# Turning q, k and x of eight head pairs by SyncE's transposing transfers instead of TensorE, with clamping sums, shared MLP sums and a new order of work

## The chip, the cores and the metric

The kernel runs on one core of one Trainium2 chip. A core has TensorE (matrix products, written to PSUM, eight banks of 2 KB per partition), VectorE, ScalarE, GpSimd and SyncE, each with an instruction queue of its own that it works off in order. In the profile they are PE, DVE, ACT, POOL and SP; PEld is TensorE's weight load. GpSimd and SyncE also issue the transfers (DMAs), which sixteen DMA engines carry out. The metric is the device time of one execution in microseconds (us).

## The reference

Windowed attention with eight global keys, followed by a token mixer of low rank and an MLP, for 4 batches, 8 heads, 768 tokens and 64 values per head:

```
scores = q @ k.T / sqrt(D) - slope[h] * dist      # keep: key < 8, or 0 <= query - key < 96
a = exp(scores - max); a = a / sum(a);  x = a @ v  # [4, 768, 512], heads side by side
u = x + (x.T @ U @ V).T                            # U is 768 x 32, V is 32 x 768
out = u + relu(u @ w_ch1) @ w_ch2                  # 512 -> 2048 -> 512
```

## The kernel before, in words

**Pairs.** The 32 heads are taken as 16 pairs p, four for each batch b (p = 4b + hp). A pair fills 128 partitions: two heads of 64 values.

**Attention of a pair** (function attention, line 578). GpSimd loads q, k and v as 16-bit numbers with tokens on the partitions (lq, lk, lv; three buffers for q and for k, four for v). TQ and TK turn q and k to values on the partitions: six 128x128 transposes each on TensorE (flip, line 611; for pairs 0 to 3 another form in line 592), into a PSUM bank. EQ and EK copy the banks to qT and kT (three buffers each), on ScalarE or VectorE as the tables "EQ" and "EK" say by a letter for each pair (A ScalarE, D VectorE, S SyncE, Q a transfer of GpSimd). KO makes kO, the keys shifted for the window, VC and VG do the same for v (SyncE for pairs 7 to 11 and 13 to 15, with one and two transfers). S forms the scores in up to three parts, EX takes exp, MK multiplies the mask, PV multiplies with v, RC and NM divide by the sum and write x as 32-bit numbers to x_sb.

**Mixer of a pair.** XC casts x to 16 bits (x16). UP (mixed, line 835) has six blocks of 128 tokens: for each, one product with the identity, which lays x transposed into two PSUM banks (line 840), and one with U of 32 columns (line 845). XE copies the 32 columns, XU turns them (line 948), TE copies them to tmp, HM (line 966) multiplies with V and adds onto the transposed x in the two banks, so that they hold u transposed. E0 copies them to uT, on the engine of table "E"; for the last pair of a batch E1 (ScalarE) and E0 (VectorE) take half each.

**MLP of a batch** (function mlp, line 995). The first product, 512 to 2048, has sixteen blocks jt of 128. Plain blocks (M1 with RL, RM) are four products of 384 or 768 columns and a relu on ScalarE. Blocks z of CFG["Z"] (4 to 7 in batches 1 and 2, 2 to 7 in batch 3) are done with block z + 8 by seven products in place of eight (ZP1 to ZP7, line 1115): ZT forms sums of uT, ZS sums of w1 (lines 1093 to 1096, four operations of 256 elements for each z, kept for z = 4 to 7, made anew in batch 3 for 2 and 3), ZU, ZW, ZX copy partial results to zu on ScalarE, ZA, ZB and ZD add a bank and such a copy on VectorE (tt, line 1133), ZR is a relu from PSUM, and ZQ and ZV are relus in place behind ZA, ZD and ZB (flat_relu, lines 1172 and 1174). The second product, 2048 to 512, is done by seven products in place of eight too: PA and PB form sums of its input (sA, two VectorE operations each, lines 1199 to 1205), RS starts three token blocks, P1 to P7 multiply (line 1246, eight products of 256 columns for each), DA, DB, DC, DD, DF and DG add banks onto x_sb (lines 1258, 1298), O stores the result (SyncE).

**What sets the order.** ORDER (line 21) names every step once, by hand. A planner (line 106) walks through it with a cost for each step, gives out buffers and PSUM banks, and sorts the steps by the start that it works out; on each engine they run in the order of the list. Semaphores between the engines follow from the data.

The lines that turn and mix x, and those that let it go on:

```
nc.tensor.matmul(ps[:, gx.slot + c // 3, ...], xx[:, c], ident16, ...)          # L840
nc.tensor.matmul(ps[:, gx.slot, 384:384 + R], xx[:, c], u16[:, c, 0], ...)      # L845
ut_done[p] = (add(e, ..., ev, [HM] + w, rel=[gx], name=f"E0{p}"),)              # copy to uT
```

## Time and profile before

| | |
|---|---|
| device time, median of 3 runs (lowest to highest) | 224.5 us (224.15 to 225.14) |
| profiled execution: span from first to last instruction | 223.0 us; the page records no other time of it |
| TensorE busy, instructions | 216.4 us, 2424 |
| VectorE busy | 181.6 us, 403 |
| ScalarE busy | 147.0 us, 260 |
| GpSimd busy | 73.7 us, 97 |
| granted TensorE clock | full throughout |
| GpSimd's transfers | 13.74 MB in 72880 packets |
| SyncE's transfers | 9.19 MB in 14496 packets |

Busy times of TensorE are of pipelined products, whose lengths overlap: six transposes of 0.22 us take 0.34 us together. In the chain of work and the timeline a merged piece therefore gives the time that its products hold TensorE, and the starts of single products give their pace. The attention of batch 0 runs from 0 to about 36 us, its MLP, mixed with the attention of batch 1, to about 80 us; the later first and second MLP products lie at 80 to 107 and 107 to 131 us (batch 1), 131 to 157 and 157 to 180 us (batch 2), 180 to 201 and 201 to 220 us (batch 3), with the attention of the next batch between.

### The profile page before, as it was taken

Reading aid. Unit: us, or ns where it says so; the run is one execution under the profiler, and the core shown is the slowest. Engines: PE = TensorE matmul, PEld = TensorE weight load, DVE = VectorE, ACT = ScalarE, POOL = GpSimd, SP = SyncE. Lnnn points to the kernel's source line nnn. Section 1 sums busy time; section 2 is a strip of 40 time slices with the busy share of each in tenths; the row PEclk is TensorE's granted clock in tenths of the full one; section 3 lists DMA queues with packets and bytes.
Section 4 is the critical chain, followed back from the end, with each engine's and each line's share of the span. In section 5 each row is a group of like instructions: output and inputs, shape, how many; then the busy total and the mean of one; then the engine's idle time right before and its main releaser. Section 6 shows DMA issues by size and latency. Waiting matters only on the chain.

```text
span 223.0 us, 5965 instructions
## 1 busy us (share of the span) xinstructions
PE 216.4 (97%) x2424; PEld 158.5 (71%) x2424; DVE 181.6 (81%) x403; ACT 147.0 (66%) x260; POOL 73.7 (33%) x97
## 2 busy tenths in 40 slices
PE   8799899999999999999999999999999999999994
PEld 3466656675879976666888876666788875658883
DVE  5688966999987987888978688597978796889872
ACT  7888798768858669788757557787742458782000
POOL 8989959714894940010851000011000000000000
PEclk9999999999999999999999999999999999999999
DMA  6999999999999997662997021409100006000025
GB/s 173 178 170 149 159 161 185 184 206 166 158 157 92 140 191 141 224 46 37 68 116 98 18 79 65 132 4 71 33 0 3 0 3 259 25 1 3 0 97 190
DMA packets 87404, 23.31 MB, mean 104 GB/s; under 512 B 73840, under 2 KB 84784, under 8 KB 87376
## 3 DMA queue, kind: packets, MB, share of 16 engines
q0 software_dynamic: 72880, 13.74, 75.6%
q1 hardware_dynamic: 14496, 9.19, 14.2%
q8 instruction: 19, 0.31, 0.6%
q14 instruction: 9, 0.07, 0.1%
HBM read 27.56 MB, written 6.29 MB: 152 GB/s over the span
## 4 chain that ended last, share of the span: by engine, by line
PE 84%; DMA 7%; POOL 5%; issue 2%; DVE 1%; ACT 0%; DVEq 0%; POOLq 0%
PE ps L1246 34%; PE ps L1115 14%; PE ps L1020 11%; PE ps L1044 7%; PE ps L734 4%; DMA vt<-in_v_dram 4%; PE ps L611 3%; DMA stgq<-in_q_dram 3%; PE ps L840 2%; PE ps L867 2%; PE ps L866 2%; POOL stgq L457 1%; POOL w L507 1%; PE ps L1238 1%; PE ps L966 1%
## 5 line engine op out<-in xcount | busy, mean ns | idle before, releaser
L799 ACT ACTIVATE ep<-ps 128x1024 f16<-128x1024 f32 (+1 forms) x48 | 44.0, 952 | 16.3 <-PE ps L734 15.1
L1246 PEld LDWEIGHTS <-htr 128*128 128x128 f16 x392 | 36.2, 98 | 6.1 <-issue 1.9
L1020 PE MATMUL ps<-uT,w 128*128 128x384 f16 x176 | 33.3, 326 | 0.0
L1258 DVE TENSOR_TENSOR x_sb<-x_sb,ps 128x256 f32<-128x256 f32 (+1 forms) x60 | 26.8, 463 | 7.6 <-PE ps L1246 7.2
L1246 PEld LDWEIGHTS <-sA 128*128 128x128 f16 x288 | 27.4, 98 | 4.2 <-issue 0.7
L461 POOL DMA_DIRECT2D vt<-in_v_dram x16 | 16.7, 1047 | 32.9 <-PE ps L867 29.7
L1026 ACT ACTIVATE htr<-ps 128x384 f16<-128x384 f32 x44 | 20.7, 493 | 5.6 <-PE ps L1020 5.3
L1246 PE MATMUL ps<-w,sA 128*128 128x256 f16 x192 | 24.2, 273 | 0.0
L1246 PE MATMUL ps<-tB,htr 128*128 128x256 f16 (+1 forms) x200 | 24.2, 268 | 0.0
L1020 PEld LDWEIGHTS <-w 128*128 128x128 f16 x176 | 16.5, 98 | 10.6
L1246 PE MATMUL ps<-w,htr 128*128 128x256 f16 x192 | 23.5, 273 | 0.0
L457 POOL DMA_DIRECT2D stgq<-in_q_dram x24 | 19.9, 852 | 5.4 <-PE ps L611 3.3
L1044 PE MATMUL ps<-uT,w 128*128 128x384 f16 x112 | 21.3, 326 | 0.0
L457 POOL DMA_DIRECT2D stgk<-in_k_dram x24 | 20.0, 852 | 2.6 <-DMA w<-in_moe_w_ch_dram 1.0
L1133 DVE TENSOR_TENSOR htr<-ps,zu 128x384 f16<-128x384 f32 x30 | 16.4, 553 | 4.7 <-PE ps L1115 3.0
L362 ACT ACTIVATE zu<-ps 128x384 f32<-128x384 f32 x30 | 14.7, 493 | 5.7 <-PE ps L1115 5.3
L812 DVE TENSOR_TENSOR ep<-ep,mask 128x1024 f16<-128x1024 f16 x24 | 16.2, 684 | 1.4 <-ACT ep L799 0.9
L905 DVE TENSOR_TENSOR x_sb<-ps,rcp 128x768 f32<-128x768 f32 x16 | 15.3, 956 | 0.9 <-DMA vo<-vt 0.4
L1044 PEld LDWEIGHTS <-w 128*128 128x128 f16 x112 | 10.7, 98 | 6.6
L1115 PEld LDWEIGHTS <-w 128*128 128x128 f16 x108 | 10.2, 98 | 6.1
L734 PE MATMUL ps<-qT,kT 64*128 64x128 f16 x192 | 14.0, 217 | 0.4 <-DVE kT L364 0.4
L1115 PE MATMUL ps<-uT,w 128*128 128x384 f16 x56 | 13.4, 326 | 0.0
(124 smaller groups left out, 450.0 us busy)
## 6 DMA issues: line engine op xcount, KB each, us to landing
out_dram<-x_sb SPq DMA_DIRECT2D x20, 256.0 KB, 2.2
vt<-in_v_dram POOLq DMA_DIRECT2D x16, 192.0 KB, 5.9
stgk<-in_k_dram POOLq DMA_DIRECT2D x24, 96.0 KB, 6.6
stgq<-in_q_dram POOLq DMA_DIRECT2D x24, 96.0 KB, 5.6
w<-in_moe_w_ch_dram POOLq DMA_DIRECT2D x8, 256.0 KB, 7.1
w<-in_moe_w_ch_dram POOLq DMA_DIRECT2D x4, 512.0 KB, 11.7
vo<-vt SPq DMA_DIRECT2D x8, 123.8 KB, 2.5
out_dram<-x_sb SPq DMA_DIRECT2D x7, 128.0 KB, 2.2
```

Of the source, the lines that this page charges most:

```text
L457: nc.gpsimd.dma_start(o[:, i], src[b, h0 + i].rearrange("(n p) d -> p n d", p=P))
L461: nc.gpsimd.dma_start(vt[gv.slot][:, :, :, 0:D], v[b, h0:h0 + 2].rearrange("h (n p) d -> p h n d", p=P),)
L734: nc.tensor.matmul(t[:, hi, j * P:(j + 1) * P], lhs, qt[r, i * P:(i + 1) * P], start=not biased, stop=True, skip_group_check=biased,)
L799: nc.scalar.activation(ep[gep.slot][:, :, lo:512], ps[:, gsc.slot:gsc.slot + 2, lo:512], AF.Exp, scale=qk_scale)
L812: nc.vector.tensor_tensor(ev, ev, mv, ALU.mult)
L1020: nc.tensor.matmul(ps[:, g.slot, 0:HS], w1[:, dc, jt * P:(jt + 1) * P], ub[:, dc, i * HS:(i + 1) * HS], start=(dc == 0), stop=(dc == NDC - 1),
L1026: nc.scalar.activation(htr[:, jt, i * HS:(i + 1) * HS], ps[:, g.slot, 0:HS], AF.Relu)
L1044: nc.tensor.matmul(ps[:, g.slot + half, 0:HS], w1[:, dc, jt * P:(jt + 1) * P], ub[:, dc, half * HS:(half + 1) * HS], start=(dc == flat[0]) ...
L1115: nc.tensor.matmul(bank(g), a()[:, i], bq[:, i], start=first and i == 0, stop=last and i == 1, skip_group_check=True,)
L1133: return lambda: nc.vector.tensor_tensor(o, x(), y(), ALU.add)
L1246: nc.tensor.matmul(o if part is None else o[:, part], a[:, j, c0 + cols.start:c0 + cols.stop], bq[:, j] if part is None else bq[:, j, part ...
L1258: nc.vector.tensor_tensor(o, o, x, ALU.add)
```

## The change

- **q and k of pairs 8 to 15** (CFG["QD"]): TQ and TK fall away; EQ and EK become one transposing transfer each, issued by SyncE from the loaded tile straight to qT or kT.
- **x of pairs 8 to 15** (CFG["XD"]): UP keeps its six products with U and loses the six with the identity. A transposing transfer XT, issued by SyncE behind XC, writes x transposed to uT. HM starts its banks afresh, and E0 (with E1 for pairs 11 and 15) adds the bank onto uT in place, always on VectorE, behind HM and XT.
- **Clamping sums**: ZA, ZB and ZD become one VectorE operation that adds and clamps from below at 0; ZQ and ZV fall away.
- **MLP sums**: ZS is made once for two blocks z (four operations of 512 elements, three steps ZS1 to ZS3), and kept; the third lies where ib and early were, so it waits for the last bias step SB.
- **PA and PB** become Sa, Sb, Sc and Sd, one operation each, and each product waits only for the one that it reads.
- **A new ORDER** and other letters in the tables of engines. Options that were switched off are taken out.

```diff
--- before.py
+++ after.py
-from concourse.masks import make_identity
+from concourse.dve_ops import TENSOR_ADD_SAT
...
 ORDER
...
+HM4 RS0.2 P20.2 E04 lv7 lk12 lq7 lq8 lv6 Sb0.3 EK7 Sd0.3 KO7 Sb0.0 lk8 lq9 lk9 VG5 Sb0.1 Sd0.0 Sd0.1 P50.0 S6.1 P20.0
+P50.2 EX6.1 PV5 EX6.2 TQ7 P30.0 P30.2 EQ7 MK6.0 VC6 RC5 NM5 lv10 S7.1 MK6.1 MK6.2 Sc0.1 DF0.2 DF0.0 P10.0 P10.2 EK8
+mask6 VG7 VC7 VG6 EQ8 XC5 EX7.2 PV6 EX7.1 RS0.1 EQ9 S7.0 DA0.0 DC0.2 TWb0 EK9 P10.1 RC6 DA0.1 DA0.2 P20.1 P50.1 P60.0
+KO8 EX7.0 MK7.1 NM6 S8.1 P30.1 P60.2 EX8.2 EX8.1 XC6 MK7.2 MK7.0 DB0.0 Sc0.3 DC0.0 DB0.2 DF0.1 UP5 PV7 RC7 XE5 NM7
+P70.2 XU5 P60.1 S8.0 TE5 HM5 DD0.2 MK8.2 E05 lq11 lv8 lk10 DB0.1 P70.0 lq10 P40.2 lk11 lq12 EX8.0 lv9 DD0.0 DC0.1 ZS2
+XC7 UP7 XE7 UP6 XE6 P70.1 XU7 DD0.1 DG0.2 XU6 TE7 P40.0 TE6 KO9 HM7 HM6 DG0.0 E17 E06 P40.1 E07 S9.1 DG0.1 EX9.1 S9.0
...
+lk13 PV10 Sb1.0 Sb1.3 DA1.1 MK11.1 DA1.0 RC10 Sd1.3 Sd1.1 NM10 Sc1.1 P61.1 P51.0 Sc1.2 VC14 P61.0 DB1.0 Sc1.0 Sd1.0
+XC10 P51.1 S12.1 VG11 VC11 P21.1 EQ14 EK14 EK13 KO14 EX12.2 XC9 P31.0 P31.1 XT8 Sc1.3 DB1.1 EX12.1 MK11.2 PV11 UP9
+P71.1 KO13 XT9 DF1.1 XE9 XU9 TE9 P71.0 lv15 RC11 VC12 NM11 DF1.0 S12.0 EX12.0 HM9 RS1.2 DD1.0 P11.2 XC11 UP8 DC1.1
+DD1.1 XE8 P41.1 E09 VG14 XT10 XT11 lv13 lk15 EK15 UP10 XU8 DA1.2 MK12.2 MK12.0 P21.2 TE8 HM8 P41.0 DG1.1 XE10 XU10 E08
+TE10 DC1.0 P61.2 UP11 HM10 P31.2 DB1.2 XE11 XU11 P51.2 E010 TE11 DG1.0 HM11 S14.1 EX14.1 EX14.2 DF1.2 E111 P71.2 E011
+ZP22.7 ZP12.4 S14.0 DD1.2 P41.2 ZP12.6 ZT2 EX14.0 ZU2.4 ZP22.4 ZA2.4 DG1.2 M1b2.5 ZP62.4 ZU2.6 ZW2.4 M1a2.4 ZP12.7
+DC1.2 MK14.0 RM2.5 MK14.1 ZP72.4 ZP62.6 ZU2.7 ZA2.7 M1a2.1 ZP52.4 M1b2.1 ZW2.6 ZX2.4 VG13 EQ13 MK12.1 KO15 ZB2.4
+ZP72.6 VG12 ZP42.4 ZP22.6 ZA2.6 RL2.4 RL2.1 ZP62.7 ZP32.4 O1.0 ZR2.4 M1a2.3 VC15 ZD2.4 TD2 M1b2.3 RL2.3 M1a2.0 M1b2.0
...
+MK15.2 Sd2.3 MK15.1 P52.2 P52.0 E012 P62.2 XT13 HM13 Sc2.1 RS2.1 MK15.0 E013 Sd2.1 Sc2.0 P62.0 P12.1 DB2.0 PV15 DA2.1
+P72.0 P32.2 RC15 NM15 XC15 P62.1 DF2.2 ZS1 P52.1 UP15 P32.0 ZP13.6 XE15 XU15 P22.1 DD2.0 DC2.1 P42.0 DB2.1 TE15 XT15
+HM15 DB2.2 E115 P72.2 DC2.0 P32.1 DG2.0 E015 P72.1 DD2.2 DF2.0 DD2.1 M1a3.1 M1b3.1 ZP13.3 P42.2 DF2.1 P42.1 ZT3 ZP13.7
+ZU3.3 RL3.1 ZU3.6 ZU3.7 ZP23.3 ZP63.6 ZP53.6 ZP23.6 ZP63.7 ZW3.6 DC2.2 ZA3.3 DG2.2 ZP63.3 ZW3.3 ZA3.6 DG2.1 ZP53.7
...
-    "ZK": (4, 5, 6, 7), "ZR": "DDADDAAD", "ZQ": "DDAADDDD", "TE": "DAADAAAADADADAAD", "XE": "DAAAAAADAAAAAAAD", "EK": "ADADDDADAADAAAAD", "EQ": "DDADAADDADADAAAA", "KO": "ADDDDDSDASASSAAD", "XC": "DDDDDQAADADAAAQA", "E": "AAAAAADAADDAAAAA"
+    "ZK": (2, 3, 1), "TE": "AAADDDAAAADAAAAD", "XE": "ADDDDAAAAAADAAAD", "EK": "ADADAADAAADAAAAD", "EQ": "DDADDDDAADADAAAA", "KO": "ADDDDDAAAAASDSAD", "XC": "DDDDDQAAAAAAAAQA", "E": "AAAADDAAADDAAAAA",
+    "TSP": 1.0, "TSZ": 1.0, "XD": (8, 9, 10, 11, 12, 13, 14, 15), "NZS": 2, "QD": (8, 9, 10, 11, 12, 13, 14, 15),
...
+    ibe = sb("ibe", [P, 2048], FP16)
+    ib = ibe[:, 0:1024].rearrange("p (h c) -> p h c", h=H)
+    early = ibe[:, 1024:2048]
...
+    NZS = CFG["NZS"]
+    zs = sb("zs", [P, NZS, 3, 2, 2 * P], FP16)
+    zh = [zs[:, i] for i in range(NZS)] + [ibe[:, 0:12 * P].rearrange("p (i a c) -> p i a c", i=3, a=2)]
...
+            if p in CFG["QD"]:
+                def turn():
+                    o = dst().rearrange("c (n p) -> c n p", n=NB)
+                    nc.sync.dma_start_transpose(o, stg[gs.slot].rearrange("p a b -> p (a b)"))
+
+                return [add(SP, TSP, turn, ld, acq=[gt], rel=[gs], size=TSZ, name=f"E{x}{p}")]
...
+                    if not turned:
+                        nc.tensor.matmul(
+                            ps[:, gx.slot + c // 3, (c % 3) * P:(c % 3 + 1) * P], xx[:, c], ident16,
+                            start=(c % 3 == 0), stop=False, skip_group_check=True,
+                        )
...
+                        ps[:, gx.slot, 384:384 + R], xx[:, c], u16[:, c],
+                        start=turned and c == 0, stop=(c == NB - 1), skip_group_check=True,
...
+            gx16.readers = 1 + turned
...
+            XT = []
+            if turned:
+                def xturn():
+                    o = uT[b % 2][:, hp].rearrange("p (n c) -> p n c", n=NB)
+                    nc.sync.dma_start_transpose(o, x16[gx16.slot].rearrange("p n c -> p (n c)"))
+
+                XT = [
+                    add(
+                        SP, TSP, xturn, [XC] + (mm1_done[b - 2] if b >= 2 else []), size=TSZ, rel=[gx16], name=f"XT{p}",
...
+                e = DVE if turned else e
+
                 def ev(half=half, e=e):
                     o, i = uT[b % 2][:, hp, half * HS:(half + 1) * HS], ps[:, gx.slot + half, 0:HS]
-                    copy(e, o, i)
-
-                ee.append(add(e, 0.5 if e == ACT else 0.55, ev, [HM] + w, rel=[gx], name=f"E{half}{p}"))
+                    if turned:
+                        nc.vector.tensor_tensor(o, o, i, ALU.add)
+                    else:
+                        copy(e, o, i)
+
+                ee.append(add(e, 0.5 if e == ACT else 0.55, ev, [HM] + w + XT, rel=[gx], name=f"E{half}{p}"))
...
+            e = DVE if turned else ENG[CFG["E"][p]]
 
             def ev():
                 o, i = uT[b % 2][:, hp].rearrange("p (h c) -> p h c", h=2), ps[:, gx.slot:gx.slot + 2, 0:HS]
-                copy(e, o, i)
-
-            ut_done[p] = (add(e, 0.81 if e == ACT else 0.95, ev, [HM] + w, rel=[gx], name=f"E0{p}"),)
+                if turned:
+                    nc.vector.tensor_tensor(o, o, i, ALU.add)
+                else:
+                    copy(e, o, i)
+
+            ut_done[p] = (add(e, 0.81 if e == ACT else 0.95, ev, [HM] + w + XT, rel=[gx], name=f"E0{p}"),)
...
+            zp, home = z // 2, zh[ZK.index(z // 2)]
+
+            def sw(i, home=home, z=z, a21=a21):
+                return a21 if i == 0 else home[:, i - 1, :, z % 2 * P:(z % 2 + 1) * P]
+
+            if zp not in kept:
+                lo2, hi2 = slice(zp * 2 * P, (zp + 1) * 2 * P), slice((zp * 2 + hj) * P, (zp * 2 + 2 + hj) * P)
+                A11, A12, A21, A22 = w1[:, 0:2, lo2], w1[:, 2:4, lo2], w1[:, 0:2, hi2], w1[:, 2:4, hi2]
+
+                def sums_s(home=home, A11=A11, A12=A12, A21=A21, A22=A22):
+                    op = nc.vector.tensor_tensor
+                    op(home[:, 1], A11, A21, ALU.subtract)
+                    op(A21, A21, A22, ALU.add)
+                    op(home[:, 0], A21, A11, ALU.subtract)
+                    op(home[:, 2], A12, home[:, 0], ALU.subtract)
+
+                free = [c_rel] + [x for n, x in pl.names.items() if n[:2] == "SB"] if ZK.index(zp) == NZS else []
+                used = [x for i in (0, 1) for x in plain_mm.get(2 * zp + i + hj, [])]
+                kept[zp] = add(DVE, 1.72, sums_s, wq + used + free, lat=0.1, fast=32, name=f"ZS{zp}")
+            ZS = kept[zp]
...
-                return lambda: nc.vector.tensor_tensor(o, x(), y(), ALU.add)
+                return lambda: nc.vector._custom_dve(TENSOR_ADD_SAT, out=o, in0=x(), in1=y(), s0=3.0e38, s1=0.0)
...
-            e1, e2 = ENG[CFG["ZQ"][z]], ENG[CFG["ZR"][z]]
-            if seeded:
-                R1 = ev("Q", e1, {ACT: 0.47, DVE: 0.26, POOL: 1.16}[e1], flat_relu(e1, quad(z, 1)), [C12], fast=1)
-            else:
-                R1 = ev("Q", e1, {ACT: 0.84, DVE: 0.4, POOL: 2.2}[e1], flat_relu(e1, htr[:, z]), [C11, C12], fast=1)
-            R2 = ev("V", e2, {ACT: 0.47, DVE: 0.26, POOL: 1.16}[e2], flat_relu(e2, quad(z + hj, 1)), [C22], fast=1)
-            relus[z], relus[z + hj] = [R1, C11], [R2, C21]
-
-        pa = []
+            relus[z], relus[z + hj] = [C11, C12], [C22, C21]
...
+            need = [r for j in js for r in relus[j]]
+
+            def one(nm, o, x, y, op, dp):
+                return add(DVE, 0.555, lambda: nc.vector.tensor_tensor(o, x, y, op), dp, fast=2, name=f"{nm}{b}.{g}")
+
+            T1 = one("Sa", s1, a21, a22, ALU.add, need + war(5))
+            T3 = one("Sc", a21, a11, a21, ALU.subtract, [T1])
+            T2 = one("Sb", s2, s1, a11, ALU.subtract, [T1] + war(6))
+            T4 = one("Sd", s4, a12, s2, ALU.subtract, [T2] + war(3))
+            for k, T_ in enumerate((T1, T2, T3, T4)):
+                pa[k].append(T_)
...
-            P6 = prod(6, gX, 0, sA[:, 1], tB[:, 0], pa[0::2] + c_tb + [DA])
+            P6 = prod(6, gX, 0, sA[:, 1], tB[:, 0], pa[1] + c_tb + [DA])
             DB = plus("DB", x12, gX, 0, [P6], rel=[gX])
-            P7 = prod(7, gX, 0, htr[:, 0:hj], tB[:, 1], pa[1::2] + c_ta + [DB], c0=HS)
...
+            P7 = prod(7, gX, 0, htr[:, 0:hj], tB[:, 1], pa[2] + c_ta + [DB], c0=HS)
```

## The prediction

> **What bounds the kernel now.** I read the page first (busy time of each engine, the 40 slices), then the stages in windows, then the chain that ended last, then the timeline of TensorE around the steps that the change touches, and last SyncE's issues with their times to landing.

> ```profile
> span 223.0 us, 5965 instructions
> ...
> PE 216.4 (97%) x2424; PEld 158.5 (71%) x2424; DVE 181.6 (81%) x403; ACT 147.0 (66%) x260; POOL 73.7 (33%) x97
> ...
> PEclk9999999999999999999999999999999999999999
> DMA  6999999999999997662997021409100006000025
> ```

> TensorE is busy for 97% at the full granted clock; the DMA engines are full until about 83 us (slice 15) and mostly free behind that. Where the missing 3% lie, the windows say (columns: stretch, length, busy time of PE, weight loads, VectorE, ScalarE, GpSimd, then clock and DMA):

> ```profile
> 0.00:40.00 40.00, 36.71 (x503) 23.18 (x504) 29.89 (x79) 32.99 (x55) 34.88 (x52) 1.00 1.73 168
> ...
> 157.00:180.00 23.00, 23.00 (x290) 19.13 (x289) 18.84 (x43) 10.43 (x16) 0.00 (x0) 1.00 0.02 4
> 180.00:201.00 21.00, 21.00 (x144) 13.07 (x141) 17.64 (x41) 15.64 (x35) 0.00 (x0) 1.00 0.20 76
> 201.00:223.00 22.00, 18.73 (x182) 16.52 (x176) 15.87 (x36) 1.17 (x2) 0.00 (x0) 1.00 0.20 73
> ```

> TensorE idles 3.3 us in the first 40 and 3.3 us after its last product; between, never. The chain of work agrees: from 36 us to 219.77 us it is a string of TensorE pieces, in which six transposes stand as a piece like any other.

> ```profile
> 37.70 0.34 PE ps L611 x6
> 38.04 0.65 PE ps L1020 x4
> 38.69 0.33 PE ps L611 x6
> ...
> 201.27 18.48 PE ps L1246 x176
> ```

> So a microsecond of TensorE work taken out between 36 and 220 us is a microsecond of the span, if the order around it keeps TensorE fed.

> **What goes from TensorE.** The q and k of pairs 8 to 15 were turned by TK and TQ (line 611): 16 steps of six transposes, 0.33 to 0.34 us each in the chain: 16 x 0.335 = 5.4 us. The x of the same pairs was turned inside UP. Its twelve products in the timeline (start, length, products):

> ```profile
> 155.13 0.22 PE L840 MATMUL ps<-ident,x 128*128 128x128 f16 x1
> 155.19 0.18 PE L845 MATMUL ps<-u,x 128*128 128x32 f16 x1
> 155.22 0.22 PE L840 MATMUL ps<-ident,x 128*128 128x128 f16 x1
> ...
> 155.62 0.48 PE L1115 MATMUL ps<-uT,zs 128*128 128x384 f16 x2
> ...
> 170.74 0.19 PE L866 MATMUL ps<-vo,ep 128*128 128x65 f16 x1
> 170.77 0.19 PE L867 MATMUL ps<-vt,ep 128*128 128x65 f16 x1
> ```

> Lengths overlap; starts count. A UP takes 155.62 - 155.13 = 0.49 us. Six 32-column products stay, each with its weight load. Alone they may cost 0.027 us each (as between the transposes here) or 0.055 us, if the neighbour hid the load; the products of line 866 and 867, each with a load of the same size, follow each other in 0.03 us, so I take 6 x 0.03 = 0.18. Saved 8 x 0.31 = 2.5 us (ends 1.3 and 2.6). Together **7.9 us** off TensorE, all between 60 and 180 us.

> **What comes to SyncE.** 24 turns of 128x768 (EK, EQ and XT of pairs 8 to 15), 196 KB each. No transposing transfer is in the trace. The nearest rows are SyncE's own copies inside SBUF (min/median/max ns of the issue; us to landing), early and late in the kernel:

> ```profile
> L366 SPq DMA_DIRECT2D vo<-vt x3: 622/638/699, 62.1 to 63.6; - x3
> ...
> DMA to landing us min/median/max: 4.9/5.0/5.3
> ...
> L366 SPq DMA_DIRECT2D vo<-vt x13: 585/612/655, 103.4 to 156.5; - x13
> ...
> DMA to landing us min/median/max: 1.9/2.0/3.9
> ```

> Call t the time that SyncE's queue spends on one turn. A copy's issue bounds it from below, 0.6 us; the longest issue of that line, 2.1 us, is the nearest row above, and nothing excludes more. I take 1.0: more work than a copy of like size, nearer to the many rows at 0.6 than to the one at 2.1. Three places matter.

> First, pair 8, which comes while loads still fill the DMA engines, where a copy lands in 5.0 us. The new order puts EK8, two transfers of VG7, one of VC7 and EQ8 in a row: EQ8 begins after 1.0 + 3 x 0.64 = 2.9 us and lands at 7.9. The order has PV6, RS0.1, S7.0 and four products of 0.87 us between EK8 and S8.1, about 4.5 us. If EK8 cannot start ahead of its place, S8.1 and all of TensorE behind it wait 3.4 us; its key slot is free since S5, so it may start as soon as its load has landed, and then nothing. I take 1.0.

> Second, the x of batch 2. From EQ14 to XT11 SyncE has seven turns and four plain transfers (KO13, VG14): 7t + 2.6 us, and 2.0 to land. TensorE has about 13 us of work listed between EQ14 and E111 (eleven products of 0.87, PV11 0.68, the UP, XU, HM, S12.0, S14.1 and RS1.2 of about 2.7). At t = 1.0 the turns are through after 11.6 us: hidden. Third, batch 3: between XC15 and E115 stand five products and the mixing, 5 us, against t + 2.0 for XT15. Hidden too. E0 now waits for HM and for XT; behind a late XT, VectorE's in-order queue holds DB and DC of the second MLP, which empty TensorE's banks.

> **VectorE and ScalarE.** Removed from VectorE: 19 clamps (12 of 0.355, 7 of 0.255: 6.1 us), four evacuations of q or k (4 x 0.56 = 2.2), two casts (1.2), and sums ZS: 24 of 0.29 become 12 of 512 elements, between the rows of 256 (0.29) and 768 (0.55), so 0.42: 6.9 - 5.1 = 1.8. Added: the u of pairs 8 and 12 to 14 and the other halves of 11 and 15. An add of 768 columns from PSUM is read from line 905, 0.956 us: 4 x 0.956 + 2 x 0.555 = 4.9. The small moves of EK, EQ, E, TE and XE among the other pairs add about 1.0. Net 5.4 us off 181.6. The 42 clamping sums: between 0 more (the same columns read, 0.553 us now) and 0.25 each (a clamp's own row); I take 0. Even 0.25 is covered: in 180 to 201 us, eighteen of them add 4.6 us, 2.2 us of clamps go, and 17.64 + 2.4 stays under 21. ScalarE loses twelve evacuations of q and k (9.7), nine clamps (5.3) and some of E (5), and gains copies of kO and casts (3.5): some 16 us lighter, nowhere the bound. Sa to Sd are the same 64 operations as before with finer waits; no wait of TensorE on sA is in the list of waits, so 0.

> **The new order** moves loads too: w1_0 stands two loads earlier in GpSimd's queue, lk12 far earlier. TensorE's idle 3.3 us in the first 40 bound the gain; for the loss I set the same size. I take 0 (ends -2 and +2).

> **The sum.** 223.0 - 7.9 + 1.0 = 216.1 us of span. The page gives the profiled execution no time but its span; the median of 224.5 lies 1.45 us over it, and I keep that: **217.5 us**, 3.1% under 224.5. About 0.5% is what a measurement of this kernel tells from no change.

> [...] The trace's own TensorE pace is 0.056 us a block. [...]

> **Rivals.**
> - *SyncE's queue becomes the bound (slower).* Place: the seven turns up to XT11. The price is 7t + 4.6 - 13: at t = 2.3 it is 7.7 us and eats the gain; that is the point from which it decides. At t = 3.0 it is 12.6: 223.0 - 7.9 + 1.0 + 12.6 + 1.45 = 230 us. For it: a turn works on 2-byte elements, and the longest issue is already 2.1. Against: 29 of 32 copies issue in 0.58 to 0.70. [...] Chance 0.14.
> - *VectorE becomes the bound in batch 2's second MLP.* In 157 to 180 us it idles 4.2 of 23. There E012, E013 and a half of 15 add 2.5 and ZS1 0.5 more than ZS3.2, which it replaces, while TensorE loses 1.2: 21.9 of 21.8. VectorE's waits on TensorE in that stretch (1.26, 0.37, 0.17, 0.65, 0.65 and 0.41 us, 3.5 in all) then find no idle to lie in: about 3 us, 220.5. Against: the order draws E014 and the masks of 13 and 15 into the stage before. Chance 0.17.
> - *The front gets better too.* Up to 2 us of the 3.3 idle, and no wait at S8.1: 214.5. Chance 0.10.
> - *Nothing arrives.* The turns go, but waits at pair 8 and at the ends of batches 2 and 3 take their place: around 224. Chance 0.05.
> - The forecast, 215.5 to 219: 0.54.

> **Chances and range.** Faster by over 0.5%: 0.54 + 0.17 + 0.10 = 0.81. Same: 0.05. Slower: 0.14. Upward the range takes in VectorE's case and the wait of 3.4 at S8.1, to the edge of no change (223.4); downward the front with its end of 2 us and a little more, 213.5. What lies outside is the SyncE case and some hundredths on each side. The forecast's own range is 215.5 to 219.

> **What will show it.** Of the 156 transposes of line 611 60 are left, of the 96 of line 840 half; TensorE's busy time falls to about 208. A turn's issue near 1 us and landings of 2 to 5 us prove the SyncE step right; over 2.3 us, wrong. No idle of TensorE before line 734 at pair 8, and none behind uT at the start of batches 2 and 3. The clamping sums stay near 0.55 us and E's adds near 0.96. Wrong it becomes if a turn keeps SyncE or lands twice as long as a copy of its size, or if VectorE shows no idle in the second MLP of batch 2.

## The result: slower, and where the time went

The changed kernel took 233.1 us (two executions, 232.9 and 233.4) against 224.6 us for the kernel before on the same chip: ratio 1.038, 95% interval 1.035 to 1.041. Forecast was 217.5 us. (Two further executions, of 237.9 and 238.8 us, were slow ones and are left out of the ratio.) The profiled execution has a span of 231.5 us, 8.4 more than before.

The page of the changed kernel (busy time of each engine; 40 slices of 5.8 us; the queue that SyncE's transfers use, as packets, MB and share of 16 engines' span):

```profile
span 231.5 us, 5638 instructions
...
PE 215.1 (93%) x2279; PEld 154.0 (67%) x2279; DVE 175.0 (76%) x374; ACT 129.8 (56%) x237; POOL 73.9 (32%) x97
...
PEclk9999999999997999976999799999999999999999
DMA  7999999999999947999969985707110122000055
...
q1 hardware_dynamic: 31072, 13.58, 25.6%
```

The granted clock, full throughout before, is dented in slices 13, 18, 19 and 23. Ahead of each dent TensorE waited, which it never did between 40 and 220 us before:

```profile
PE ps L895 <- DMA vo<-vt: 4.8, 1, 4.8
PE ps L768 <- DMA qT<-stgq: 2.5, 1, 2.5
PE ps L896 <- ACT ep L833: 1.0, 1, 1.0
...
PE ps L879 <- ACT ep L833: 0.8, 1, 0.8
```

This view counts a wait from the modelled end of the last product, about 0.16 us later than the usual distance to the next start; the waits in the list below are counted from that distance and so are a little longer (4.95 for 4.8, 2.67 for 2.5).

The windows show wait and dent side by side (columns as in the prediction; the clock is the third number from the end):

```profile
66.00:71.00 5.00, 2.49 (x28) 2.04 (x27) 4.40 (x9) 0.79 (x2) 1.64 (x2) 0.98 2.17 167
71.00:74.20 3.20, 3.20 (x28) 2.33 (x25) 0.00 (x0) 2.33 (x3) 1.65 (x2) 0.50 1.54 160
...
98.00:101.50 3.50, 0.00 (x0) 0.00 (x0) 0.43 (x1) 0.81 (x3) 2.29 (x3) 1.00 1.75 175
101.50:108.30 6.80, 5.62 (x44) 3.31 (x46) 2.68 (x5) 1.44 (x3) 3.02 (x4) 0.50 1.96 188
108.30:125.50 17.20, 17.20 (x214) 13.28 (x209) 14.49 (x30) 10.13 (x16) 3.69 (x4) 1.00 1.03 101
```

The chain of work, unbroken TensorE before, now goes through three transfers of SyncE's queue, and ends as before in the same last block of 18.48 us:

```profile
64.93 5.74 DMA qT<-stgq
...
98.43 4.21 DMA vo<-vt
...
119.88 5.30 DMA kT<-stgk
...
208.67 18.48 PE ps L1264 x176
```

These are the three places.

- *S8.1, at 70.8 us: 2.67 us.* The turn of q of pair 8 is issued at 64.93, behind EK8 and three copies of v, and lands 5.74 us later. 3.4 us at half clock follow.
- *PV8, at 102.7 us: 4.95 us.* The copy VC8 is issued at 98.43. Ahead of it on SyncE stand the turns of k and q of pairs 10 to 12, eight transfers of v (pairs 8 to 10) and five stores. 6.8 us at half clock follow.
- *PV11 and UP9, near 128 us: 1.2 and 1.0 us.* ScalarE stands 3.1 us before KO14, which needs the turn of k of pair 14, and the exponentials of pair 12 are behind it. 3.4 us at half clock follow.

I split each span as follows. In the trace of the kernel before, the median distance from a product's start to the next is 55 ns for 128 columns, 109 for 256 and 162 for 384. On the line through these a product of N columns is counted as N / 2.4 + 3 ns (half for the paired products of 64 rows or 64 columns: two of them start 3 ns apart there, and the next two mostly some 0.05 us later for 128 columns, 0.11 for 256); whatever a start comes later than that is "lost", half clock included; what lies behind the last start is the tail (0.9 us ahead of the first start are not shown).

| kernel | span | TensorE's work | lost | tail |
|---|---|---|---|---|
| before | 223.0 | 204.3 | 14.4 | 3.5 |
| changed | 231.5 | 196.1 | 29.9 | 4.5 |

So the work fell by 8.2 us, 0.3 more than forecast, and 15.6 us of lost time and 1.0 of tail ate it. The waits of the three places are 9.8 us; of the 13.7 us at half clock TensorE worked 12.4, at about twice the usual time (213 ns from start to start for 256 columns, 320 for 384), so 6.2 us are lost there. Together 16.0; in other places the changed kernel loses a little less than before.

### The profile page after: what moved, and what is told of

The parts are those of the page before. It is cut to its first block, busy times and chain, and to the rows that moved or that the text cites. A ratio compares the mean times of both kernels' runs of the same rounds, so it can differ in the third digit from the quotient of the medians.

```text
span 231.5 us, 5638 instructions
## 1 busy us (share of the span) xinstructions
PE 215.1 (93%) x2279; PEld 154.0 (67%) x2279; DVE 175.0 (76%) x374; ACT 129.8 (56%) x237; POOL 73.9 (32%) x97
## 3 DMA queue, kind: packets, MB, share of 16 engines
q1 hardware_dynamic: 31072, 13.58, 25.6%
## 4 chain that ended last, share of the span: by engine, by line
PE 70%; DVE 13%; DMA 8%; SPq 3%; ACT 3%; issue 2%; DVEq 0%; ACTq 0%
PE ps L1264 26%; PE ps L1166 12%; PE ps L1072 10%; PE ps L1096 6%; PE ps L768 4%; DVE sA L1226 3%; DMA qT<-stgq 2%; DMA kT<-stgk 2%; PE ps L896 2%; DMA vo<-vt 2%; PE ps L749 2%; PE ps L895 2%; DVE ep L846 2%; DVE x_sb L934 2%; SPq L653 1%
## 5 line engine op out<-in xcount | busy, mean ns | idle before, releaser
L833 ACT ACTIVATE ep<-ps 128x1024 f16<-128x1024 f32 (+1 forms) x48 | 43.7, 953 | 14.5 <-PE ps L768 14.4
L1264 PEld LDWEIGHTS <-htr 128*128 128x128 f16 x392 | 36.7, 100 | 7.2 <-issue 1.8
L1072 PE MATMUL ps<-uT,w 128*128 128x384 f16 x176 | 34.3, 331 | 0.1
L1264 PEld LDWEIGHTS <-sA 128*128 128x128 f16 x288 | 28.2, 100 | 4.3 <-issue 0.6
L500 POOL DMA_DIRECT2D stgq<-in_q_dram x24 | 20.0, 843 | 21.4 <-DMA qT<-stgq 20.8
L1264 PE MATMUL ps<-tB,htr 128*128 128x256 f16 (+1 forms) x200 | 25.8, 280 | 0.0
L1264 PE MATMUL ps<-w,sA 128*128 128x256 f16 x192 | 24.8, 279 | 0.0
L1072 PEld LDWEIGHTS <-w 128*128 128x128 f16 x176 | 16.6, 99 | 11.2 <-issue 1.2
L504 POOL DMA_DIRECT2D vt<-in_v_dram x16 | 16.6, 1036 | 23.1 <-PE ps L896 19.9
L1096 PE MATMUL ps<-uT,w 128*128 128x384 f16 x112 | 21.3, 326 | 0.1
L1183 DVE CUSTOM_DVE_ANT_0 htr<-ps,zu 128x384 f16<-128x384 f32 x30 | 16.1, 554 | 5.8 <-PE ps L1166 5.3
L405 ACT ACTIVATE zu<-ps 128x384 f32<-128x384 f32 x30 | 14.0, 497 | 10.7 <-PE ps L1166 9.7
L895 PE MATMUL ps<-vo,ep 128*128 128x65 f16 x160 | 12.2, 196 | 5.5 <-DMA vo<-vt 4.8
L1166 PEld LDWEIGHTS <-w 128*128 128x128 f16 x112 | 11.1, 100 | 7.1 <-issue 0.7
L768 PE MATMUL ps<-qT,kO 64*128 64x128 f16 x160 | 13.1, 225 | 2.6 <-DMA qT<-stgq 2.5
L1096 PEld LDWEIGHTS <-w 128*128 128x128 f16 x112 | 10.6, 98 | 6.9 <-issue 0.3
```

Of the source, the lines that this page charges most:

```text
L500: nc.gpsimd.dma_start(o[:, i], src[b, h0 + i].rearrange("(n p) d -> p n d", p=P))
L768: nc.tensor.matmul(t[:, hi, j * P:(j + 1) * P], lhs, qt[r, i * P:(i + 1) * P], start=not biased, stop=True, skip_group_check=biased,)
L833: nc.scalar.activation(ep[gep.slot][:, :, lo:512], ps[:, gsc.slot:gsc.slot + 2, lo:512], AF.Exp, scale=qk_scale)
L895: nc.tensor.matmul(o, e[:, hi, j * P:(j + 1) * P], vof[:, hi, i - 1, 0:D1], start=True, stop=False)
L1072: nc.tensor.matmul(ps[:, g.slot, 0:HS], w1[:, dc, jt * P:(jt + 1) * P], ub[:, dc, i * HS:(i + 1) * HS], start=(dc == 0), stop=(dc == NDC - 1),
L1096: nc.tensor.matmul(ps[:, g.slot + half, 0:HS], w1[:, dc, jt * P:(jt + 1) * P], ub[:, dc, half * HS:(half + 1) * HS], start=(dc == flat[0]) ...
```

## The experiments

Theory A: SyncE's queue, which works in order (in the changed kernel it issues nothing between 69.75 and 80.95 us but the two stores at its head), is what is late. Rivals: the turns land late wherever they are issued (B, and D for the DMA engines' load); the new order is worse as such (C, E).

**One place mended at a time.** Four reorderings of the changed kernel, no instruction added or dropped.

```diff
# q8
-EK8 mask6 VG7 VC7 VG6 EQ8
+EK8 EQ8 mask6 VG7 VC7 VG6
# vo8
-EK12 VG9 VG10 ... EQ12 VG8 O0.2 ZR1.4 ZP71.7 ZP11.6 VC8
+EK12 VG8 VC8 VG9 VG10 ... EQ12 O0.2 ZR1.4 ZP71.7 ZP11.6
# ko14
-EK13 KO14 EX12.2 ... S12.0 EX12.0
+EK13 EX12.2 ... S12.0 EX12.0 KO14
# three: all of these
```

> One edit to the kernel after: EQ8 stands directly behind EK8 in the order, ahead of VG7 and VC7, so on SyncE's queue the turn of q of pair 8 passes three issues. Theory A (SyncE's in-order queue is what is late; each long wait of TensorE is followed by a stretch at half clock that costs about as much again): the wait of S8.1 at 70.8 us, 2.67 us long, falls to 0 or nearly, the half-clock stretch of 3.4 us behind it goes too, and the span falls by 2.7 + 1.7 = 4.4 us, from 231.5 to about 227. Rival B (the transposing transfers themselves land late, wherever they are issued): the wait stays and the span stays at 231 to 233. Rival C (the new order is slower as a whole, and the waits are only where its slack comes to light): the wait goes, but a later one grows by as much, span 230 to 232.

> One edit to the kernel after: the two copies of v of pair 8 (VG8, VC8) are issued by SyncE ahead of those of pair 9 and of EQ10 to EQ12, that is in the place of VG9. Theory A: PV8's wait at 102.7 us, 4.95 us long, falls to under 1 us, the half-clock stretch of 6.8 us behind it shrinks with it, and the span falls by 4.2 to 8 us, to 224 to 227. Rival B: the copies land late because the DMA engines are full there, PV8 still waits 3 us or more, span 229 to 232. Rival C: PV8 does not wait but S10 or PV9 does, for the turns that now go later; span 230 to 232.

> One edit to the kernel after: KO14, the offset copy of k of pair 14 on ScalarE, stands behind EX12.0 instead of ahead of the exponentials of pair 12. Theory A: ScalarE no longer stands 3.12 us at 125.2 us for the turn of k of pair 14, TensorE's two waits of 1.2 and 1.0 us near 128 us and the 3.4 us at half clock behind them go, span lower by 2.2 to 3.9 us: 227.6 to 229.3. Rival B: ScalarE was not what held TensorE, the waits stay and the span is 231 to 232.

> The edits of q8, vo8 and ko14 together. Theory A: the three sums add up, 12 to 15.6 us in all, span 216 to 219.5 and time 217.5 to 221, faster than the kernel before (224.5): the part of the forecast on TensorE's work was right and three places in SyncE's queue cost more than it. Rival B (landing times): 229 or more. Rival C: new waits take the place of the three, span 223 to 229.

Measured spans: 233.3, 230.6, 237.8 and 235.1 us; ratios to before 1.041 (1.032 to 1.050) for q8, 1.061 (1.052 to 1.070) for ko14, 1.056 (1.046 to 1.065) for all three. For vo8 there is no ratio: its two executions, 232.5 and 240.4 us, lie too far apart. None came near theory A's sum. In q8 the turn of q left at 63.54, 1.4 us earlier, and landed 8.86 us later: S8.1 waited 2.9 us, and PV8 7.0 by the view (4.8 in the changed kernel). In vo8 the copies of v came in time, and the next thing in the queue was late; its chain of work:

```profile
97.10 1.29 SPq L653
98.50 1.23 SPq L653
99.78 0.60 SPq L1317
...
100.43 5.05 DMA out_dram<-x_sb
105.56 0.97 DVE x_sb L934
106.57 0.61 PE ps L768 x8
```

Two turns and a store stand ahead of another store, on which NM8 (line 934) waits, since it overwrites what is stored; S10.1 waits for NM8. In ko14 the wait of ScalarE went, and TensorE waited 4.9 us at 138 us for u instead, behind a turn of x that took 6.99 us to land. So the wait stays and changes its name: no one entry is what is late. That is B and C as much as A. Nor do single waits of 1 or 2 us more or less tell much: ko14 is the changed kernel up to about 120 us, and yet by the view S8.1 waited 3.3 us and PV8 6.4 in its profiled execution (2.5 and 4.8 in the changed kernel's). The four reorderings do not decide between the theories.

**What of a turn is dear.** In the next two kernels the 24 turns are plain copies at the same places; the second cuts each copy into small pieces.

```diff
# plain
-                    nc.sync.dma_start_transpose(o, stg[gs.slot].rearrange("p a b -> p (a b)"))
+                    nc.sync.dma_start(dst(), stg[gs.slot].rearrange("p a b -> p (a b)"))
# chop
+                    nc.sync.dma_start(o[:, :, 0:126], stg[gs.slot].rearrange("p a b -> p (a b)").rearrange("c (n p) -> c n p", n=NB)[:, :, 0:126])
# the same for x in xturn
```

> The kernel after, with each of its 24 transposing transfers replaced by a plain copy of the same bytes on the same queue, at the same place (the heads are then not turned, so that the output is not the reference's: q, k and x of pairs 8 to 15 enter the products unturned). What four reorderings showed before: a wait taken away in one place came back in another (spans 230.6 to 237.8), and turns landed up to 8.5 us after their issue between 60 and 72 us. Theory A (only the order in SyncE's queue and the number of its issues count): issues fall from 1.2 to about 0.65 us each, 24 x 0.6 = 14 us off SyncE's queue, but the landing stays at 4 to 8 us; the waits near 70, 102 and 127 us stay in part, span 226 to 231. Theory D (turning itself loads the DMA engines: a turn adds some 690 small packets, 16,576 in all, 11 points of the 16 engines' time): landing falls under 4 us, the waits fall to less than half and with them the half-clock stretches, span 217 to 223. Rival E (the new order as such): 230 or more.

> The kernel with plain copies again, but each cut into rows of 252 bytes: 126 of the 128 columns of each of the six blocks are copied, so that a copy has 768 small pieces, about as many packets as a turn has (691), and nothing is turned (the heads are not turned and two columns of each block keep old values, so the output is not the reference's). Theory D1 (a turn costs through its many small packets): issue, landing and waits are those of the kernel after, hardware queue near 25 per cent of the engines' time, span 229 to 233. Theory D2 (turning itself is what is slow, not the number of packets): span near the 220.6 us of the whole copies, 219 to 223, and landing under 4 us.

The turns of q and k, their issue (min/median/max ns) and their landing, first in the changed kernel, then with whole copies, then with chopped ones:

```profile
L653 SPq DMA_TRANSPOSE kT<-stgk x8: 1210/1237/1337, 60.3 to 135.7; - x8
L653 SPq DMA_TRANSPOSE qT<-stgq x8: 1215/1315/2123, 64.9 to 143.6; - x8
...
  POOL stgq L500: 20.8, 3
...
DMA to landing us min/median/max: 2.7/4.0/6.5
```

```profile
L652 SPq DMA_DIRECT2D kT<-stgk x8: 465/516/1106, 61.1 to 126.1; - x8
L652 SPq DMA_DIRECT2D qT<-stgq x8: 468/539/549, 65.2 to 132.9; - x8
...
DMA to landing us min/median/max: 2.1/2.3/5.6
```

```profile
L653 SPq DMA_DIRECT2D kT<-stgk x8: 593/646/1732, 61.6 to 131.0; - x8
L653 SPq DMA_DIRECT2D qT<-stgq x8: 605/652/960, 65.9 to 137.2; - x8
...
DMA to landing us min/median/max: 2.7/3.9/6.3
```

Whole copies: span 220.6 us, 0.9985 of before (0.994 to 1.003). Chopped: 226.0 us, 1.013 (1.008 to 1.018). Turns: 231.5 us, 1.038. The work of TensorE is 196.1 us in all three, so nearly all of the 10.9 us between the ends is lost time. From whole to chopped, 5.4 us, the landing rises to that of a turn (2.3 to 3.9 us), with issues only 0.12 us longer: I read these as the price of landing in small packets, 784 a copy instead of 144 (a turn has 800). From chopped to turned, 5.5 us, the landing stays (3.9, 4.0) and the issue nearly doubles (0.65 to 1.24 us): I read these as SyncE's longer issues. The second reading is not isolated, since the queue's share of the engines' time rises too, from 23.1% to 25.6%. The ratios give 3.3 and 5.5 us for the two steps; the profiled execution with whole copies, 222.5 us, is the shortest of its nine. D1 and D2 were each right in part. At the median a turn lands no later than a copy in as many pieces; what it has of its own is the issue.

(The packets are the counts of the queue with turns, chopped and whole copies and without any, 31072, 30688, 15328 and 11872, as differences over 24 transfers. The 16,576 more than before, and the 690 or 691 a turn of the expectations, are net: the change also took four transfers of shifted keys, 2,624 packets, off this queue.) The line of GpSimd is the same matter from another side: its loads of q waited 20.8 us for buffers that the turns had not yet freed.

Note also that even whole copies, which turn nothing, only draw level: they still wait 2.8 us at S8.1 and 1.9 at PV8.

**Parts taken back.** Three kernels gave q and k, x, or both back to TensorE.

```diff
# noq: "QD": (), TK and TQ put beside EK and EQ in the order, some EK and EQ moved with them
# nox: "XD": (), XT8 to XT15 dropped from the order
# neither: both
```

> The kernel after without its first part: q and k of pairs 8 to 15 go back to TensorE's transposes and evacuations by ScalarE and VectorE; x keeps its turns on SyncE; the order is that of after with each TK, TQ beside its EK, EQ. Theories A and D: TensorE gets 16 x 0.335 = 5.4 us of work back, and the waits at 70.8 and 102.7 us with their half-clock stretches go (4.4 and 8 us): span 231.5 + 5.4 - 12.4 = about 224.5, within 222 to 227. Rival E: the waits stand in other places and the span is 231 to 237.

> The kernel after without its second part: x of pairs 8 to 15 is turned by TensorE in its products again, and VectorE does not complete u in place; q and k keep their turns. Theories A and D: TensorE gets 8 x 0.31 = 2.5 us back; the waits at 70.8 and 102.7 us stand, since they lie before the first turn of x; those at 127 us stay or shrink, span 230 to 234. Rival E: no change beyond the 2.5 us, span 234.

> The kernel after without either part: no transposing transfer is left, the clamping sums, the single MLP sums and the new order are. Theories A and D: TensorE's work is that of before, the waits of TensorE are the 14 us of before or a little more, and the span is 223 to 227: the turns, and not the sums or the order, made the kernel slower. Rival E: 230 or more without any turn: the order or the sums cost it.

Ratios 1.058 (1.048 to 1.067), 1.049 (1.040 to 1.058), 1.057 (1.048 to 1.066). For nox, 235.5 and 236.6 us of time are a span near 234, which fits A and D (230 to 234) and E (234) alike; for A and D speaks that TensorE's work rises by 2.7 us and that the waits of S8.1 and PV8, both ahead of the first turn of x, stay (4.1 and 6.1 us in the profiled execution, whose span is 238.2). The other two came out as rival E had it: 235 to 241 us for noq (A and D: 222 to 227, E: 231 to 237) and 234.7 to 237.3 for neither (A and D: 223 to 227, E: 230 or more). My own order explains a part of that. I had put the transposes where the turns had been issued, and TensorE, which works in order too, stood there for a load (2.9 us in noq) and for exponentials that ScalarE did late behind the evacuations (3.2 us in both). The rest stays open. Against E as the cause in the changed kernel speaks the kernel with whole copies, which has the changed kernel's order and is level with before, where E had 230 us or more. The order is made for the turns, and these three are no measure of the kernel without them.

**Work in the wait.**

```diff
             def pv_all(steps=tuple(PVs)):
+                for _ in range(80 if p == 8 else 0):
+                    nc.tensor.matmul(ps[:, gpv.slot, 0:P], ident16, ident16, start=True, stop=True, skip_group_check=True)
```

> The kernel after, with 80 products of 128 columns ahead of the products of P and v of pair 8 on TensorE, into the same bank; they wait for nothing that is late and their result is overwritten. They take 80 x 0.056 = 4.5 us and so stand in the wait of 4.95 us at 102.7 us. If the half clock after a long wait is part of the loss: the 6.8 us at half clock behind that wait go, the span falls by about 3.4 us to 228, though work was added. If the half clock has another cause (the DMA traffic, say): the stretch at half clock stays and the span stays at 231.5 or rises.

Span 239.1 us, ratio 1.067 (1.060 to 1.074). Neither expectation holds. The stretch at half clock behind PV8 shrank from 6.8 to 3.4 us, but PV8 still waited 2.9 us behind the filler, S8.1 3.7 and a product behind u 3.6 us later on, each with half clock after it (mean granted clock of that execution 0.964, against 0.970 in the changed kernel). This run alone does not give the price of the half clock; how much idle time lay ahead of it in two traces is told at the end.

**The other transfers off the queue.** Here the turns stay and the copies of v of pairs 7 to 11 go to ScalarE.

```diff
-    "VO": "DDDDDDASSSSSDSSS",
+    "VO": "DDDDDDAAAAAADSSS",
 # and in the order some VG and VC of pairs 7 to 11 change places among themselves
```

> The kernel after, with the offset copies of v of pairs 7 to 11 made by ScalarE instead of by SyncE's transfers (VC and VG of these pairs): 15 issues of 0.6 us and their packets leave SyncE's queue, and the turns meet less there; ScalarE gets 5 x 1.48 = 7.4 us, in a stretch where it is 60 to 70 per cent busy. Theory A (the queue's order and its issues): PV8's wait at 102.7 us (4.95 us and the half clock behind it) goes, S8.1's wait at 70.8 us shrinks by the 2.2 us of three issues: span 231.5 - 8 - 2 = 221.5, within 219 to 225. Rival (landing times alone): the stores or the turns themselves are waited for in their place, span 228 to 233.

Span 224.1 us, ratio 1.010 (1.007 to 1.013): 7.4 us of the 8.4 are back by an edit that touches no turn. TensorE's waits:

```profile
PE ps L768 <- DMA qT<-stgq: 2.5, 1, 2.5
PE ps L1166 <- ACT zu L405: 1.5, 2, 1.4
PE ps L620 <- DMA stgq<-in_q_dram: 1.2, 2, 0.9
```

PV8's wait is gone, the clock is full throughout (1.0). Theory A's forecast (219 to 225) holds, though its median turn still lands after 3.8 us: a late landing hurts where something waits for it, and the queue decides how many do. S8.1 waits as before; the turns of pairs 8 and 9 land there after 5.9 to 9.0 us, while the packets' time adds up to 2.0 times the engines' time between 60 and 70 us (packets overlap). The 2.2 us of issues that I took away ahead of EQ8 bought nothing: its issue took 2.85 us.

To see whether that last wait belongs to the turn, the last kernel of this line gave pair 8 back to TensorE:

```diff
 # on top of the one before
-    "QD": (8, 9, 10, 11, 12, 13, 14, 15),
+    "QD": (9, 10, 11, 12, 13, 14, 15),
-EK8 mask6 ... VG6 EQ8 ... RS0.1
+mask6 ... VG6 TQ8 EQ8 ... RS0.1 TK8 EK8
```

> voA, and q and k of pair 8 alone go back to TensorE and ScalarE (the other 22 turns stay). Theory (the turns of pair 8 are late because GpSimd's loads keep the DMA engines busy between 60 and 70 us): S8.1's wait of 2.66 us goes, TensorE gets 0.67 us back, span 224.1 - 2.0 = 222.1, time near 224.5. Rival (S8.1 is simply due too early in the new order): it waits 2 us or more for something else, span 224 to 227.

Span 225.7 us, ratio 1.015 (1.012 to 1.018). The span is the rival's: S8.1 itself waits only 0.9 us for ScalarE's evacuation, and the products of line 896 ahead of it 1.8 us, by the profile for a transfer of x, 2.7 us together. With the turn or without it, something is due too early there.

**The same turns on the kernel before, where the DMA engines have room.** The code of the turns, in the kernel before, for pairs 12 to 15 alone, in the places of TK and TQ between 97 and 140 us.

```diff
# bq
+            if p in CFG["QD"]:          # (12, 13, 14, 15); EK and EQ stand where TK and TQ stood
+                return [add(SP, 1.0, turn, ld, acq=[gt], rel=[gs], size=1.0, name=f"E{x}{p}")]
# bqx: and "XD": (8, 9, 10, 11, 13, 14, 15), each XT behind its XC
```

> The kernel before, with one part of the change in a stretch where its DMA engines have room: q and k of pairs 12 to 15 alone are turned by SyncE's transposing transfers, at the place where TensorE's TK and TQ of these pairs stood, between 100 and 130 us; all else is before's, its order too (KO15 goes behind EQ15). TensorE loses 8 x 0.335 = 2.7 us, VectorE and ScalarE eight evacuations. Theory D (turns cost where they meet GpSimd's loads on the DMA engines): hardly a wait is added, span 223.0 - 2.7 = 220.3, time 221.8, within 220.5 to 223.5. Rival (turns cost wherever they stand, by SyncE's queue and by landing): 225 or more.

> As the one before it, and x of pairs 8 to 11 and 13 to 15 turned too, each turn right behind its XC in before's order, u completed by VectorE in place. TensorE loses 2.7 + 7 x 0.31 = 4.9 us. Theory D: span 218.1 to 220.5, time 219.5 to 222, faster than both kernels. Rival: the turns of x land too late for u and hold VectorE's queue, whose in-place sums stand at the places of the copies; span 223 or more.

bq: ratio 1.007 (1.003 to 1.010), that is 225.1 to 227.7 us; the profiled execution took 229.4 us (span 227.6), longer than those. In it TensorE's work fell by the forecast 2.7 us, and two waits of PV took 4.4; how long they were in the others is not known. The queue around them (start, length, transfers):

```profile
109.74 1.22 SPq L624 DMA_TRANSPOSE qT<-stgq  x1
111.06 1.41 SPq L365 DMA_DIRECT2D kO<-kT  x2
112.52 1.73 SPq L365 DMA_DIRECT2D vo<-vt  x2
114.36 1.98 SPq L624 DMA_TRANSPOSE kT<-stgk  x1
...
117.48 1.26 SPq L365 DMA_DIRECT2D vo<-vt  x2
```

EQ14 stood at the head of the queue for 8.0 us until a buffer of qT was free, and the copies of v for PV11 and PV10 behind it. bqx: span 228.3 us, 1.037 (1.029 to 1.045), the rival's case: VectorE's in-place sums stand in order where the copies stood, and wait for turns to land.

```profile
PE ps L874 <- DMA vo<-vt: 3.4, 1, 3.4
PE ps L739 <- DVE uT L1009: 1.9, 1, 1.9
PE ps L1136 <- DVE uT L1009: 1.6, 1, 1.6
...
PE ps L1259 <- DVE uT L1009: 0.7, 1, 0.7
```

Then the two turns of pair 14 were moved behind the copies that they had held, and with them KO14, ScalarE's copy of the turned keys; bq2x adds x of pairs 8 to 11, bq3 adds q and k of pair 11.

```diff
# bq2
-EQ14 ... TE9 MK11.2 MK11.1 VG11 PV11 lk14 EK14 lk15 ... KO14 ... VG12 ... VG10
+TE9 MK11.2 MK11.1 VG11 PV11 lk14 lk15 ... VG12 ... VG10 EK14 EQ14 ... XE11 KO14
# bq2x: "XD": (8, 9, 10, 11), each XT behind its XC, E08 to E011 and E111 some places later
# bq3: "QD": (11, 12, 13, 14, 15), EK11 and EQ11 where TK11 and TQ11 stood, KO11 later
```

> The kernel before with q and k of pairs 12 to 15 turned by SyncE, as before, but the turns of pair 14 stand behind VG11, VG12 and VG10 in SyncE's queue instead of ahead of them (and KO14 later). Theory (a turn costs through what stands behind it in the queue, and where the DMA engines have room only through that): the two waits of PV near 119 and 121 us (2.5 and 2.0 us) and the half clock behind them go; span 227.6 - 4.4 - 1.7 = 221.5, time near 222.5, 0.9 per cent faster than before. Rival: another wait of 2 us or more comes in their place, time 225 or more.

> As the one before it, and x of pairs 8 to 11 turned by SyncE too, each right behind its XC, its completion by VectorE four places later in the order. Theory: 4 x 0.31 = 1.2 us more off TensorE, time near 221.5. Rival: the four turns of x (1.2 us of SyncE each, between 105 and 130 us) stand ahead of v's copies, or VectorE waits for them in order: time 224 or more.

> bq2, and q and k of pair 11 turned by SyncE too, where TensorE's TK11 and TQ11 stood, near 82 to 85 us; KO11 20 places later. TensorE loses 0.67 us. If a turn is free wherever nothing behind it in the queue is due: time 223.1 - 0.7 = 222.5. If the 2.5 us of issues delay the copies of v of pair 8 behind them (stores and copies fill the queue from 85 to 96 us): PV8 waits 1 to 2.5 us, time 223.5 to 226.

bq2: 223.1 us, ratio 0.993 (0.991 to 0.996), span 221.6; bq3: 223.5 us, 0.995 (0.992 to 0.997). Both are faster than the kernel before, by under 1%, and than the changed one. In bq2 no wait is left that the kernel before does not have in like size:

```profile
PE ps L1368 <- POOL zero L378: 0.9, 1, 0.9
PE ps L739 <- DVE kT L363: 0.7, 1, 0.7
PE ps L591 <- DMA stgk<-in_k_dram: 0.6, 2, 0.3
```

Its work is 2.7 us below before and its lost time 1.2 above. So a turn can be free: two entries of a queue and one copy, moved, are 1.3% of the time, from a loss to a gain. bq3's two turns near 85 us cost PV8 nothing; their 0.7 us do not show, since the front lost about as much (1.1 us near 43 us for weights). bq2x: 229.3 us, 1.020 (1.017 to 1.023), again its rival: TensorE waits 1.9 us at 108 us for VectorE's sum behind a turn of x, and more at 132 and 138.

The main kernels in one table (profiled executions, us; half clock without the very end of the kernel; ratios as above).

| kernel | span | work | lost | half clock | ratio to before |
|---|---|---|---|---|---|
| before | 223.0 | 204.3 | 14.4 | 0 | 1 |
| changed | 231.5 | 196.1 | 29.9 | 13.7 | 1.038 |
| whole copies | 220.6 | 196.1 | 19.1 | 0 | 0.9985 |
| chopped copies | 226.0 | 196.1 | 23.9 | 3.4 | 1.013 |
| v's copies on ScalarE | 224.1 | 196.1 | 23.0 | 0 | 1.010 |
| before + turns of 12 to 15 (bq) | 227.6 | 201.6 | 21.6 | 3.4 | 1.007 |
| the same, pair 14 later (bq2) | 221.6 | 201.6 | 15.6 | 0 | 0.993 |

## Why the prediction was wrong, step by step

- *What goes from TensorE: right.* Forecast 7.9 us, measured 8.2. A UP with x turned takes its six products in 0.16 us:

```profile
133.88 0.30 PE L879 MATMUL ps<-u,x 128*128 128x32 f16 x6
...
134.90 0.30 PE L879 MATMUL ps<-u,x 128*128 128x32 f16 x6
```

  (0.30 is five starts 0.027 us apart and the last one's length; the sum had 0.18.)
- *What comes to SyncE: the step that failed.* t was 1.24 us, not 1.0, well inside its bounds and far below the 2.3 at which the rival was to decide; the size of t is not the miss. The miss is "Three places matter". The list held two places where a turn's result is due, pair 8 and the x of batch 2, and a third at the end. It had none for what stands *behind* the turns in the same queue. The largest loss, 4.95 us and its half clock, is PV8 waiting for VC8, an instruction that the change does not touch, with six turns, eight transfers of v and five stores ahead of it. From 81.12, where a store leaves the queue's head, to 99.05 SyncE issues without a pause. To walk that list with the forecast's 1.0 us a turn puts VC8 at 98.43 - 6 x 0.24 = 97.0 and, with the forecast's 2.0 us to land, its landing at 99.0; PV8 was due at 97.7. So the walk alone would have shown a wait of 1.3 us. Of the rest, 1.4 us are the turns' longer issues and 2.2 the longer landing (4.21 us), a second term that was too small. Two stores that waited for VectorE at the queue's head, from 69.8 to 80.6 us, had also put off what follows; no run moved these. What it is worth to relieve the queue, three runs show (spans): with whole copies in the same places 220.6 us and with v's copies on ScalarE 224.1, both for 231.5; with the two turns of bq and KO14 moved back 221.6 for 227.6.
- *First place, pair 8: the wait and its bounds were right, the value taken was not.* It had the wait between 0 and 3.4 us; 2.67 came, and 1.0 was taken. EQ8 was to land 7.9 us after EK8's issue; it landed after 10.4 (60.28 to 70.67).
- *Second place, x of batch 2: hidden from TensorE's x, but not from k.* XT11 was in time. The turn of k of pair 14 in the same row held ScalarE 3.1 us through KO14, two waits of 1.2 and 1.0 us. KO14 had not been looked at as a reader of a turn.
- *Third place: right.* No wait stands at XT15.
- *A cost that the sum had no term for:* the half clock behind the waits, 6.2 us by the count above.
- *VectorE and ScalarE: right.* The clamping sums cost what plain ones do, 554 ns against 553, E's sums 949 ns (0.956 forecast). VectorE's busy time fell by 6.6 us, ScalarE's by 17. The rival "VectorE becomes the bound" did not come: in the second MLP of batch 2, at 167 to 190 us here, it is busy 21.38 of 23 us and TensorE is busy throughout.

```profile
L1183 DVE CUSTOM_DVE_ANT_0 htr<-ps,zu 128x384 f16<-128x384 f32 x30 | 16.1, 554 | 5.8 <-PE ps L1166 5.3 <-ACT htr L1211 0.4
```

- *The front: about 0,* and the tail 1.0 us longer, which was not forecast.
- *The rival "SyncE's queue becomes the bound"* (0.14, 230 us) had the right resource and nearly the time. It looked for it in the wrong place and made it hang on t alone. With landings of 2.3 us and issues of 0.5, below the smallest t considered (0.6), the kernel was still only level with before.

What stays open: the loss in noq and neither is only partly that of my own placing, so the new order without turns has no price, and a rival that finds a part of the loss in it is weakened by the whole copies, not refuted. How the cost of a turn divides between landing and issue (5.4 and 5.5 us by single profiled executions, 3.3 and 5.5 by the ratios) is not shown either.

## What to carry to other kernels

Work moved from a saturated engine to a queue that works in order, as SyncE's did here (in bq one entry held it for 8.0 us), is priced by walking that queue to the end: for every entry, touched or not, when it is now issued and who waits for it, with engines that reach the queue through a third one included. Put a transfer that may have to wait for a buffer behind those that can go. Then move only what finds room: eight turns well placed in the order of the kernel before gained 0.7%, twenty-four in a new order lost 3.8%.

## What the runs showed of the hardware

*Landing and packets.* On this queue a turn of q or k, 196 KB in 800 packets, landed in 2.7 to 6.5 us in the changed kernel, and in up to 9.0 with v's copies on ScalarE, issued between 60 and 76 us, where the packets' time adds up to 2.0 times the engines' time (60 to 70 us); 784 packets, chopped, landed in 2.7 to 6.3 us; the same bytes in whole rows, 144 packets, in 2.1 to 5.6. With the 24 turns the queue's share of the engines' time rose from 14.2% to 25.6%; with whole copies of the same bytes it is 19.6%.
